# Another written order for a fused attention and expert kernel's first stage, and 21 small operations on another engine

## The chip, the cores and the metric

The kernel runs on one core of one Trainium2 chip. The metric is the device time of one execution in microseconds (us). A core has five engines with a queue each: TensorE (PE; its weight loads are PEld), VectorE (DVE), ScalarE (ACT), GpSimd (POOL) and SyncE (SP, which here only issues transfers). A queue runs in order: an instruction that waits holds up all behind it on its engine, and engines wait for one another through semaphores.

## The reference

Three steps follow one another, all in 32-bit floats.

```python
scores = scale * x @ state.T; a = softmax(scores); xread = a @ state        # B 4, H 8, S 512, Ns 32, D 64
scores2 = scale * state @ x.T; a2 = softmax(scores2); sread = a2 @ x
x = concat(xread, sread)                                                    # 2176 rows of 512
e = argmax(x @ w_gate); g = softmax(x @ w_gate)[e]                          # 8 experts, capacity 576
out = g * (relu(x @ w1[e]) @ w2[e])                                         # D 512, F 1024, rows over capacity give 0
h = out @ w_in; result = (h * clip(h + 3, 0, 6) / 6) @ w_out                # F 2048
```

## The kernel before

**Stages.** The function phase1 (line 72) is the first stage: attention, the choice of experts, the lists of rows for each expert, and, woven in, the first tile of 256 rows of the first expert. Then full (line 600) goes through the other expert tiles, with weights loaded as the routing asks for them, and at last through the dense layers (w_in, w_out), the longest stage. Every product of the expert and dense layers is made as three products of a high and a low part: the high part is a cast on ScalarE, the low part is the value minus the high part, on DVE or POOL.

**The first stage's parts.** Tiles are named by batch b (0 to 3) and half f (0, 1: four heads each). A part is a Python generator, and one step of it issues one or a few instructions:

- tr (269) turns x on TensorE and evicts it on ScalarE; scores (280) multiplies with the state into PSUM.
- soft_max (286) and turn (302) read the scores on DVE, soft_exp (296) on ScalarE. read_max (305) takes a maximum on DVE and subtracts it (L313: POOL, or DVE where ALT has sub), read_exp (315) is ScalarE's, read_sum (318) makes three DVE steps and a multiplication (L326: POOL, or DVE with mul in ALT). read_turn (328) turns the result on DVE.
- e2_turn (331), s_read (341), s_scale (357), s_turn (366) and s_logits (374) make sread and its logits. read (395) makes xread, evicted by ScalarE or, with rd in ALT, by DVE (L403). rows_out (407) adds up the logits and writes the rows to memory.
- count, total, sums, before and place (414 to 518) find each row's expert and its place in the list. first_expert (444) gives the index by which the first weights are loaded. before has one POOL copy (L513) ahead of two DVE sums.
- lists (520) makes, for five groups of rows of a batch, a pair of one-hot matrices: ol on DVE or ScalarE, oh (L538) on POOL or, with oh in ALT, on DVE. lists2 (542) multiplies the five pairs on TensorE (L544) and adds the result to the list LT on DVE.
- The parts that start with e_ (lines 941 to 1012) are the first expert tile: e_rows gathers its rows through two POOL transfers as soon as batch 0's list is there, e_x0 and e_x1 turn them, e_m0 to e_m3 are the first layer (L903, then ScalarE L907 and DVE L909), e_y0 and e_y1 the second (L921, then the product with the gate on DVE, L931, and the write to y_pad on SP, L937). w00 to w13 (L824, L826) split the first expert's eight weight blocks: a cast on ScalarE, then the low part on DVE or, with wp in ALT, on POOL.
- raws (835) loads these eight blocks on SP into four buffers, so the second four wait for the first to be used up. tables (662) and halves (711) are long rows of small DVE operations which say which tile belongs to which expert. inputs, setup0 to setup3, consts and zeros load and fill constants.

**What sets the order.** ORDER (line 29) is a list of part names, written out. Line 569 goes through it: each name advances that part by one step (name*3 by three), so it fixes the order of the instructions in each engine's queue. ALT (line 66) names the operations that go to the other of two engines.

**Behind the first stage** SP reads the tables and issues weight loads under conditions, POOL gathers the next tile's rows (L1133, L858) through the list, and TensorE turns them (L846). Where two tiles have one expert the load is left out.

Of the kernel before, what the change touches and what calls it, by code (L numbers as in the profile page):

```python
# [28 lines left out]
ORDER = """
    setup0 inputs setup0*4 tr00 prep_state0 tr01 tr00 setup2 setup3 prep_state0*2 tr01 scores00 setup2 tr02 setup3 setup2 setup0 tr03 setup2 setup0  # L30
    setup1 tr02 prep_state2 setup2*2 tr03 setup1*2 inputs*2 prep_state2 setup2*2 inputs prep_state2 soft_max00 prep_state2 scores01 prep_state2 tr10
    prep_state2 setup3*2 prep_gate soft_exp00 setup2 zeros turn00 read_max00 setup2*2 read_max00 setup2*2 read_exp00 soft_max01 turn01 setup2 setup3
    tr11 setup2*2 tr10 setup1 tr11 setup2 soft_exp01 read_max01 prep_gate e2_turn00 scores10 read_sum00 consts tr12 e2_turn00 s_read00 setup2
    e2_turn01 tr12 read_sum00*2 tr13 s_read00 setup2 soft_max10 read_max01 e2_turn01 tr13 s_read00 scores11 turn10 read_exp01 read_sum00 soft_exp10
    tr20 read_max10 inputs setup2 tr20 setup2 read_turn00 setup2*2 setup3 setup2 read_init0 read_sum01*2 soft_max11 read_sum01 read_init1 s_read01
    setup2 s_scale0 read06 read04 read_max10 turn11 read_exp10 soft_exp11 s_scale0 read_max11 tr21 tr22 tr21 read_sum01 scores20 setup3 tr23 s_read10
    read_sum10 setup3 s_read10 consts setup2 tr22 read04 read_sum10 e2_turn10 read_sum10 tr23 setup3 read_turn01 read_max11 read00 read_sum10 read06
    s_turn0 setup3 scores21 soft_max20 read_exp11 turn20 s_ids0 read05 read_turn10 read00 read_max20 turn21 read05 setup3 s_turn0 setup3 read_max20
    read_sum11 read01 read07 read01 read02 e2_turn10 read07 read03 soft_max21 s_logits0 read02 read03 read_exp20 read_max21 rows_out0 s_logits0 early
    read_sum11 count0 rows_out0 read_sum20 count0 e2_turn11 read10*2 count0 s_logits0 tr30 read_sum20 setup3 s_read10 e2_turn11 read_max21 count0 tr31  # L40
    setup3 s_scale0 setup3 read_sum11 setup3 count0 consts before0 setup3 tr30 read14 read_sum11 first_expert soft_exp20 read_exp21 first_expert tr31
    read_sum20 consts before0 read12 first_expert s_scale1 e2_turn20 read_sum21 first_expert*2 scores30 read_turn11 first_expert setup3 count0
    s_read11 setup3 first_expert before0 read_sum21 soft_exp21 s_read20 tr32 first_expert read_sum21 read15 read14 first_expert*2 raws total0 read12
    s_scale1 e2_turn20 tr32 soft_max30 s_read20 sums0 read13 place0 raws place0 e2_turn21 turn30 place0 read_sum21 read_turn21 s_turn1 read_sum20
    read13 tr33 place0 read_max30 raws read15 first_expert place0 e2_turn21 read16 read_turn20 place0 tr33 total0 place0 raws read_max30 place0
    s_read20 soft_exp30 s_scale2 read_init2 read11 scores31 s_logits0 s_turn1 place0 read17 lists0 e2_turn30 s_read21 read11 lists0 read16 read17 w00
# [1577 lines left out]
```

## Time and profile before

| | |
|---|---|
| median of 3 runs | 563.12 us (562.98 to 563.13) |
| the profiled execution | 564.15 us |
| its span | 562.4 us |
| mean granted TensorE clock | 0.978 of full speed |
| TensorE busy | 532.6 us, 95% of the span |
| DVE busy | 309.0 us, 55% |
| ScalarE busy | 218.0 us, 39% |
| POOL busy | 144.5 us, 26% |

A busy time is the sum of an engine's instructions. The span is the time from the first to the last instruction; the execution's own time has a little more around it. A share over the whole span is a mean over stages with different limits, so the rows further down are taken from stretches.

### The profile page before, as it was taken

Reading aid. Unit: us, or ns where it says so; the run is one execution under the profiler, and the core shown is the slowest. Engines: PE = TensorE matmul, PEld = TensorE weight load, DVE = VectorE, ACT = ScalarE, POOL = GpSimd, SP = SyncE. Lnnn points to the kernel's source line nnn. Section 1 sums busy time; section 2 is a strip of 40 time slices with the busy share of each in tenths; the row PEclk is TensorE's granted clock in tenths of the full one; section 3 lists DMA queues with packets and bytes.
Section 4 is the critical chain, followed back from the end, with each engine's and each line's share of the span. In section 5 each row is a group of like instructions: output and inputs, shape, how many; then the busy total and the mean of one; then the engine's idle time right before and its main releaser. Section 6 shows DMA issues by size and latency. Waiting matters only on the chain.

```text
span 562.4 us, 10121 instructions
## 1 busy us (share of the span) xinstructions
PE 532.6 (95%) x3772; PEld 466.5 (83%) x3772; DVE 309.0 (55%) x729; ACT 218.0 (39%) x461; POOL 144.5 (26%) x198
## 2 busy tenths in 40 slices
PE   5898899899999999999999999999999999999990
PEld 3566698796969898999998889999999998888880
DVE  3799978428735774676788953343334343222330
ACT  5577553225304250524444343333333343323340
POOL 1554645401610110117768732001001000000002
PEclk9798889999999999999999999999999999999997
DMA  6825730896989795336664312001001010000001
GB/s 136 184 103 218 247 111 20 281 401 232 374 283 401 251 377 174 98 113 226 224 209 148 115 37 76 1 23 53 1 19 58 1 31 19 20 0 1 0 13 57
DMA packets 52169, 74.99 MB, mean 133 GB/s; under 512 B 23089, under 2 KB 31537, under 8 KB 51602
## 3 DMA queue, kind: packets, MB, share of 16 engines
q1 hardware_dynamic: 49634, 66.83, 35.4%
q0 software_dynamic: 2208, 7.38, 3.9%
q8 instruction: 32, 0.52, 0.4%
q14 instruction: 23, 0.19, 0.1%
q10 hardware_dynamic: 272, 0.07, 0.1%
HBM read 70.62 MB, written 16.23 MB: 154 GB/s over the span
## 4 chain that ended last, share of the span: by engine, by line
issue 38%; PE 31%; DMA 15%; DVE 11%; ACT 3%; POOL 1%; POOLq 0%; SPq 0%; DVEq 0%; ACTq 0%
PE pm L921 8%; PE pm L903 7%; DMA out_dram<-o,fid 7%; DMA raw<-in_moe_w_dram 3%; DMA st<-in_moe_w_out_dram 3%; PE psX L400 2%; PE pm L1252 2%; PE p L1286 2%; PE pss L284 2%; PE pss L903 2%; DVE v L1096 1%; PE psx L276 1%; DVE g L1299 1%; DVE v L1094 1%; DVE v L1092 1%
## 5 line engine op out<-in xcount | busy, mean ns | idle before, releaser
L1286 PE MATMUL p<-yT,wh 128*128 128x256 f32 (+1 forms) x768 | 116.7, 294 | 0.0
L1286 PEld LDWEIGHTS p<-yT,wh 128*128 128x128 f32 x768 | 109.3, 188 | 7.8
L1299 DVE SCALAR_TENSOR_TENSOR g<-u,p 128x256 f32<-128x256 f32 x110 | 44.9, 409 | 111.0 <-ACT u L1298 110.9
L1298 ACT ACTIVATE u<-p,b 128x256 f32<-128x256 f32 x110 | 51.1, 464 | 103.4 <-PE p L1286 103.3
L1300 ACT CAST gh<-g 128x256 fp32r<-128x256 f32 x110 | 43.9, 399 | 79.9 <-DVE g L1299 79.9
L1464 POOL DMA_INDIRECT out_dram<-o,fid x14 | 14.0, 1000 | 215.9 <-ACT o L1463 190.8
L1286 PE MATMUL p<-yT,wl 128*128 128x256 f32 (+1 forms) x384 | 66.8, 296 | 0.9 <-POOL wl L1111 0.9
L1324 PE MATMUL po<-wh,gh 128*128 128x512 f32 x156 | 61.2, 392 | 0.0
L1324 PE MATMUL po<-wh,gl 128*128 128x512 f32 x156 | 61.2, 392 | 0.0
L1324 PE MATMUL po<-wl,gh 128*128 128x512 f32 x156 | 61.0, 391 | 0.0
L1286 PEld LDWEIGHTS p<-yT,wl 128*128 128x128 f32 x384 | 55.4, 189 | 2.6 <-POOL wl L1111 1.7
L1306 DVE TENSOR_TENSOR gl<-g,gh 128x256 fp32r<-128x256 f32 x84 | 34.4, 410 | 32.2 <-ACT gh L1300 32.2
L903 PE MATMUL pm<-xth,w1h 128*128 128x256 f32 x160 | 44.6, 283 | 1.8 <-ACT xth L849 1.5
L921 PE MATMUL pm<-hth,w2h 128*128 128x256 f32 x160 | 45.5, 284 | 0.0
L921 PE MATMUL pm<-hth,w2l 128*128 128x256 f32 x160 | 45.1, 282 | 0.0
L921 PE MATMUL pm<-htl,w2h 128*128 128x256 f32 x160 | 45.1, 282 | 0.0
L903 PE MATMUL pm<-xth,w1l 128*128 128x256 f32 x160 | 43.6, 277 | 0.0
L1111 POOL TENSOR_TENSOR wl<-v,wh 128x1024 fp32r<-128x1024 f32 x14 | 34.4, 2454 | 35.4 <-ACT wh L1110 35.0
L903 PE MATMUL pm<-xtl,w1h 128*128 128x256 f32 x160 | 41.6, 277 | 0.0
L1324 PEld LDWEIGHTS po<-wh,gl 128*128 128x128 f32 x156 | 29.3, 188 | 7.0 <-POOL gl L1306 0.6
L903 PEld LDWEIGHTS pm<-xth,w1h 128*128 128x128 f32 x160 | 30.1, 188 | 5.1 <-issue 2.9
L1306 POOL TENSOR_TENSOR gl<-g,gh 128x256 fp32r<-128x256 f32 x26 | 25.1, 967 | 30.6 <-ACT gh L1300 30.6
(307 smaller groups left out, 1029.1 us busy)
## 6 DMA issues: line engine op xcount, KB each, us to landing
raw<-in_moe_w_dram SPq DMA_DIRECT2D x80, 512.0 KB
st<-in_moe_w_in_dram SPq DMA_DIRECT2D x16, 512.0 KB
st<-in_moe_w_out_dram SPq DMA_DIRECT2D x16, 512.0 KB
x_rows<-xrow SPq DMA_DIRECT2D x4, 1072.0 KB
xb<-in_x_dram SPq DMA_DIRECT2D x32, 128.0 KB
yg<-y_pad SPq DMA_DIRECT2D x13, 258.0 KB
out_dram<-zt SPq DMA_DIRECT2D x2, 1536.0 KB
y_pad<-y SPq DMA_DIRECT2D x5, 516.0 KB
```

Of the source, the lines that this page charges most:

```text
L284: T.matmul(ps[64 * a:64 * a + 64, :], sT[:, 2 * b + f, 64 * a:64 * a + 64], st[b]["xT"][:, 2 * f + a], start=True, stop=True)
L400: T.matmul(ps, s["aT"][:, f, j, :], bd[:, 2 * b + f, :], start=True, stop=True)
L903: T.matmul(ps[:, j], W1[l][k][:, ls], xT[r][:, k], start=n == 0, stop=n == 11)
L921: T.matmul(ps[:, j], W2[l][k // 2][:, k % 2, ls], hT[k // 2][r][:, k % 2], start=k == 0 and i == 0, stop=k == 7 and i == 2)
L1111: (V if m in (0, 2) else G).tensor_tensor(out=wl, in0=v, in1=wh.bitcast(F32), op=ALU.subtract)
L1286: T.matmul(out, w[:, 128 * k:128 * k + 128], r(k), start=n == 0, stop=n == 11)
L1298: A.activation(out=u, in_=ps, func=AF.Relu, bias=b3)
L1299: V.scalar_tensor_tensor(out=g, in0=u, scalar=6.0, in1=ps, op0=ALU.min, op1=ALU.mult)
L1300: A.copy(gh[:, 0:w], g)
L1306: eng.tensor_tensor(out=gl, in0=g[:, 0:n], in1=gh[:, 0:n].bitcast(F32), op=ALU.subtract)
L1324: T.matmul(po[t], l[:, ls], r[:, 512:1024], start=m == 0 and i == 0, stop=m == 15 and i == 2)
L1464: G.indirect_dma_start(out=out, out_offset=bass.IndirectOffsetOnAxis(ap=fid[0:n, t:t + 1], axis=0), in_=o[0:n], in_offset=None, bounds_che ...
```

## The change

ORDER is written anew from the first word to the last; every part occurs as often as before. ALT changes in 21 names. From DVE to POOL go the multiplications mul11 and mul30, the subtraction sub30 and the one-hot rows oh01, oh12, oh20 and oh34. From POOL to DVE go mul21, sub10, oh04, oh31 and the low parts of w01, w03 and w11 (wp). From DVE to ScalarE go the evictions rd10, rd17, rd21, rd31 and rd37; from ScalarE to DVE go rd01 and rd27. Here are the lines of it that are spoken of below:

```diff
@@ -27,45 +27,44 @@
 SCALE = 0.125
 
 ORDER = """
-    setup0 inputs setup0*4 tr00 prep_state0 tr01 tr00 setup2 setup3 prep_state0*2 tr01 scores00 setup2 tr02 setup3 setup2 setup0 tr03 setup2 setup0
-    setup1 tr02 prep_state2 setup2*2 tr03 setup1*2 inputs*2 prep_state2 setup2*2 inputs prep_state2 soft_max00 prep_state2 scores01 prep_state2 tr10
-    prep_state2 setup3*2 prep_gate soft_exp00 setup2 zeros turn00 read_max00 setup2*2 read_max00 setup2*2 read_exp00 soft_max01 turn01 setup2 setup3
-    tr11 setup2*2 tr10 setup1 tr11 setup2 soft_exp01 read_max01 prep_gate e2_turn00 scores10 read_sum00 consts tr12 e2_turn00 s_read00 setup2
...
-    read27 lists0 s_logits1 s_scale1 read_exp30 lists0 read24 lists0 read27 read25 lists0 rows_out1 s_scale2 turn31 soft_max31 lists0*2 s_ids2
-    soft_exp31 s_logits1 read_max31 s_turn2 read26 read25 lists0 count1 lists0*3 read24 first_expert lists20 count1 read26 read_sum30 consts read23
-    lists20 s_read30 count1 read_max31 read20 e_rows read_exp31 read_sum30 s_read30 e2_turn31 s_turn2 read23 e2_turn30 count1 read20 e_rows read_sum30
-    read21 e2_turn31 count1 read_sum31 rows_out1 before1 read_sum30 s_read30 s_logits2 read_sum31 count1 w01 read_turn30 consts read22 read_init3
...
-    read30 w02 read33 s_scale3 read31 e_x0 read36 e_x1 e_x0 s_scale3 e_ok before1 s_turn3 place1 read35 read33 rows_out2 total1 read37 raws count2
-    before1 count2 e_g s_turn3 w01 e_x1 s_logits1 read36 w03 s_logits1 e_x1 read37 s_logits3 read35 s_logits3 place1 count2 rows_out3 e_m0 count2
-    place1 count2 e_m0 place1 e_m0 count3 e_m0 place1 count3 e_m1 e_g place1*2 w10 count2 e_m0 s_logits2 place1*2 count3 total2 e_m0 before2 count3
-    before2 count3 total2 lists1 e_m0 s_ids3 count3 lists1*2 e_m1*2 total3 sums3 before2 before3 total3 raws lists1 before3 lists1 e_g sums2 before3
-    w10 lists1 e_m1 totals e_m0 place2 tables e_m1*2 e_m2 lists1 e_g place3 rows_out2 lists1 e_m2*3 e_ok e_m2 place2 tables place2 lists1 place2 e_m1
...
-    place2 e_m3 halves w13 lists2 place2 halves w11 w13 e_y1 lists2*5 s_scale2 e_ok tables halves lists21 e_y1 lists2 halves e_y0 place3 lists2 halves
-    lists2*2 tables halves lists2 tables e_y0*3 halves lists2 e_y0 tables halves place3 lists22 lists3*2 halves*2 lists3 tables lists3 e_g halves
-    lists3*2 e_y0 s_logits2 lists3 halves lists3 e_y1 lists22 e_y0 s_logits3 lists3*2 halves*2 lists3*2 tables halves lists3 e_g halves tables*2
-    lists23*2 halves e_gt*2 e_y1 halves e_y0 e_y1 halves e_y0 e_y1*2 halves e_y1 halves*3 e_y1*2
+    setup0*2 inputs tr00 setup0*4 tr01 setup0 tr00 prep_state0 setup2 setup1 setup2 prep_state0 zeros tr01 setup2 consts*2 setup2*2 prep_state0 setup1
+    inputs prep_state2 scores00 tr02 setup1 inputs tr02 setup2 tr03 tr10 setup2 tr03 setup3 setup2*2 scores01 prep_state2 soft_max00 tr11 prep_state2
+    turn00 read_max00*2 tr10 turn01 read_max01 prep_state2 setup3 soft_exp00 soft_max01 e2_turn00 tr11 setup2 read_exp00 prep_state2 setup3 e2_turn00
+    read_sum00 scores10 soft_exp01 soft_max10 read_max01 setup3*2 read_exp01 prep_state2 tr12 setup1 tr13 setup2 prep_gate tr12 tr13 read_sum00 inputs
...
+    read10 s_ids1 read_exp30 read10 place0 first_expert place0 turn31 e2_turn21 place0*3 read13 place0 s_turn1 s_logits1 s_logits0 total0 e2_turn21
+    s_logits1 read13 lists0 place0*2 soft_exp30 read15*2 read11 lists0 s_read20 read11 s_read21 read_sum21 rows_out1 lists0 soft_exp31 lists0*3 read26
+    s_scale2 read_max31 consts raws count1 read_max31 e2_turn30 read_turn21 read26 lists0 read_sum30 raws lists0 read_exp31 lists0 count1 read_sum30
+    lists0 rows_out1 s_scale2 s_logits0 e2_turn31 s_read30 read25 lists0 read27 count1 s_scale1 read24 read_sum30 read25 lists0 read_sum30 s_ids2
+    read_sum31 lists20 read27 lists20 e2_turn31 read24 read23 read22 s_read30 w00 read23 s_turn2 read22 read_sum31 e_rows s_read31 count1 read20
+    read21 e2_turn30 e_rows read_turn30 s_turn2 read_init3 s_read30 count1 read_sum31 s_logits2 w02 count1 read_sum31 read20 before1 read32 w00
...
+    total1 raws count2 s_scale3 consts e_x0 w01 s_logits1 e_x0 read35 e_x0 s_turn3*2 e_g before1 count2*2 e_x1 before1 read34 read36 rows_out2
+    s_logits3 place1*2 read35 read37 e_x1 s_logits3 count2 e_x1 s_logits1 w03 count2 place1 read33 w03 w10 place1*2 count2 read33 e_m0 total2 e_m1*2
+    read36 e_m0 before2 e_m0 read37 sums2 e_m0 w10 rows_out3 e_m0 e_g total2 place1 count3 place1 e_m0 count3*2 place2 before2 count3 e_m1 place1 e_ok
+    first_expert w12 e_m1 e_m0 e_g count3 lists1 e_m1*2 count3 before2 before3*2 e_g total3 place2 total3 e_m0 totals sums3 raws w12 e_m2 place3
+    lists1 e_g place1 before3 e_g s_logits3 e_m2 place2 e_m2 place2 tables raws place2 e_m1 tables lists1 w11 e_m2 e_m1 e_m2 place3 e_g e_m2 w11 e_m3
+    s_ids3 place3 tables e_m3 s_logits2 e_g lists1 e_m3 lists1 e_m3 tables lists1 e_m2 place2 lists1*2 tables e_m3 lists1*2 tables halves tables
...
+    s_scale2 s_logits3 lists2*4 e_y0 lists2 lists21 lists2 e_y1 place3 halves lists2 halves e_y1 tables halves lists2 tables place3 e_y1 tables
+    lists2*4 place3 e_y1 halves lists22 tables halves lists3 s_logits2 halves lists22 halves tables e_y0 lists3 halves lists3 halves lists3 halves
+    lists3 tables halves e_y0 e_y1 lists3*6 halves tables halves lists3 tables lists3 lists23 e_y1 halves*2 rows_out3 lists23 e_gt e_y0 halves*2 e_y0
+    tables s_scale3 halves e_y1 halves e_y0 e_y1 e_y0 e_y1 halves e_y1 halves
 """
 
 
 ALT = frozenset("""
-    mul11 mul30 mul31 oh01 oh12 oh20 oh30 oh32 oh34 ol01 ol02 ol10 ol11 ol12 ol21 ol22 ol30 ol33 ol34 rd10 rd17 rd21
-    rd31 rd37 sub30 wp01 wp03 wp11
+    mul21 mul31 oh04 oh30 oh31 oh32 ol01 ol02 ol10 ol11 ol12 ol21 ol22 ol30 ol33 ol34 rd01 rd27 sub10
 """.split())
```

Read from left to right, some places differ as follows. turn00 stands ahead of soft_exp00, where it stood behind it. scores01 stands behind tr10, where it stood ahead of it. Between read_max31 on DVE and the one-hot row ol03 stand read_turn21 and the first step of read_sum30. read_sum31's first step stands ahead of e_rows. On POOL the multiplication of read_sum30 stands ahead of e_rows' two transfers. On DVE w00, w02 and w01 stand ahead of the low parts of e_x0 and e_x1, and w03 behind them; w12 and w11 follow between the first layer's parts. On POOL before2 and before3 stand ahead of all one-hot rows of lists1 to lists3, so that twelve of these follow one another. On TensorE lists21 stands ahead of e_y0's first step, and lists22 and lists23 between steps of e_y0 and e_y1.

## Rows read from the trace of the kernel before

**Rows 1.** Stretches: length, busy us of PE, PEld, DVE, ACT, POOL (instructions); PEclk, DMA share, GB/s

```profile
14.00:57.00 43.00, 39.24 (x433) 26.35 (x432) 37.83 (x115) 30.81 (x77) 22.82 (x63) 0.88 0.56 168
...
67.50:98.50 31.00, 30.06 (x223) 29.17 (x221) 25.53 (x128) 13.54 (x28) 14.20 (x26) 0.90 0.28 96
98.50:128.50 30.00, 27.22 (x224) 25.58 (x224) 11.29 (x22) 8.74 (x15) 6.19 (x12) 1.00 0.95 338
128.50:562.00 433.50, 420.10 (x2784) 374.75 (x2780) 218.70 (x437) 152.25 (x316) 91.03 (x69) 0.99 0.34 117
```

**Rows 2.** Chain of waits, 57 to 129 us: start, length, what

```profile
61.07 4.40 DVE w1l L826 x2
...
67.58 7.12 PE pss L903 x36
...
95.52 3.53 DMA xg<-x_rows,col
...
118.04 10.31 DMA raw<-in_moe_w_dram
```

**Rows 3.** Timeline of SP's queue: start, length, instruction, count

```profile
101.39 0.39 SPq L937 DMA_DIRECT2D y_pad<-xb  x1
...
105.12 13.25 SPq L814 DMA_DIRECT2D raw<-in_moe_w_dram  x16
```

**Rows 4.** Waits of DVE, 9.49 to 53.6 us: total, times, longest

```profile
DVE R L303 <- ACT e L300: 3.1, 1, 3.1
DVE m L294 <- PE pss L284: 1.8, 2, 1.4
DVE rs L320 <- ACT R L316: 0.8, 1, 0.8
DVE rr L348 <- ACT e L300: 0.7, 2, 0.4
DVE t L485 <- PE bank L478: 0.6, 1, 0.6
```

**Rows 5.** Timeline of PE, 11 to 14 us: start, length, instruction [idle before, releaser]

```profile
11.06 1.22 PE L284 MATMUL pss<-xT,sT 128*64 128x512 f32 x4
13.29 0.63 PE L276 MATMUL psx<-identk,xb 128*128 128x128 f32 x4 [1.01 <-DMA xb<-in_x_dram]
```

**Rows 6.** Timelines of DVE and POOL: long operations beside one another

```profile
50.65 1.85 DVE L536 TENSOR_SCALAR ol<-io,lo,idmi 32x128 fp32r<-32x128 f32 x1
...
57.81 2.64 DVE L439 TENSOR_TENSOR Gs<-Gs,O 128x8 f32<-128x8 f32 x1
...
82.34 1.78 DVE L718 SCALAR_TENSOR_TENSOR Q<-Q,c 128x8 f32<-128x8 f32 x1
...
58.07 2.35 POOL L826 TENSOR_TENSOR w1l<-raw,w1h 128x1024 fp32r<-128x1024 f32 x1
```

**Rows 7.** Groups by line, 0 to 98.5 us: count, busy us, mean ns, idle before

```profile
L826 DVE TENSOR_TENSOR w2l<-raw,w2h 128x1024 fp32r<-128x1024 f32 x3 | 3.7, 1222 | 0.0
...
L326 POOL TENSOR_TENSOR R<-R,rs 128x512 f32<-128x512 f32 x5 | 5.2, 1049 | 5.7 <-ACT xT L278 2.1 <-DVE Gs L465 1.8 <-DVE rs L324 1.3
...
L326 DVE TENSOR_TENSOR R<-R,rs 128x512 f32<-128x512 f32 x3 | 2.1, 685 | 0.0
...
L538 POOL TENSOR_SCALAR oh<-io,hi 128x144 fp32r<-128x144 f32 (+1 forms) x14 | 11.0, 794 | 7.7 <-DVE hi L507 3.2 <-DVE Q L657 2.6 <-DVE s L747 1.0
...
L538 DVE TENSOR_SCALAR oh<-io,hi 128x144 fp32r<-128x144 f32 (+1 forms) x6 | 2.1, 354 | 0.0
```

**Rows 8.** Timelines of PE at 86 us and of DVE at 100 us

```profile
86.15 0.38 PE L921 MATMUL pss<-xb,w2h 128*128 128x256 f32 x1 [0.77 <-DVE xb L909]
...
100.60 0.69 DVE L931 TENSOR_TENSOR xb<-pss,gB 128x512 f32<-128x512 f32 x1 [3.38 <-PE pxt L846]
```

**Rows 9.** Timelines of DVE and POOL around 54.6 us

```profile
54.66 0.68 DVE L326 TENSOR_TENSOR R<-R,rs 128x512 f32<-128x512 f32 x1
...
54.58 1.28 POOL L858 DMA_INDIRECT xb<-x_rows,ecol  x1 [2.16 <-PE psX L400]
```

More of the change, by code (lines that the diff above doesn't have):

```diff
@@ L34 @@
[L34 to L45, printed above, removed]
@@ L50 @@
-    read21 e2_turn31 count1 read_sum31 rows_out1 before1 read_sum30 s_read30 s_logits2 read_sum31 count1 w01 read_turn30 consts read22 read_init3
-    read22 read34 read_sum31 w02 read21 read32 read_sum31 read32 s_ids1 read30 read34 s_logits2 total1 read_turn31 w00 s_read31 sums1 e_x0 w03 read31
-    read30 w02 read33 s_scale3 read31 e_x0 read36 e_x1 e_x0 s_scale3 e_ok before1 s_turn3 place1 read35 read33 rows_out2 total1 read37 raws count2
-    before1 count2 e_g s_turn3 w01 e_x1 s_logits1 read36 w03 s_logits1 e_x1 read37 s_logits3 read35 s_logits3 place1 count2 rows_out3 e_m0 count2
@@ L58 @@
-    e_g*2 e_m3 e_m2 e_m3 raws halves consts e_m2 tables e_ok s_logits3 w11 place3 halves s_scale3 lists1 place3 e_m3 lists21 tables halves tables
-    place2 e_m3 halves w13 lists2 place2 halves w11 w13 e_y1 lists2*5 s_scale2 e_ok tables halves lists21 e_y1 lists2 halves e_y0 place3 lists2 halves
-    lists2*2 tables halves lists2 tables e_y0*3 halves lists2 e_y0 tables halves place3 lists22 lists3*2 halves*2 lists3 tables lists3 e_g halves
-    lists3*2 e_y0 s_logits2 lists3 halves lists3 e_y1 lists22 e_y0 s_logits3 lists3*2 halves*2 lists3*2 tables halves lists3 e_g halves tables*2
@@ new lines @@
+    read_sum00 scores10 soft_exp01 soft_max10 read_max01 setup3*2 read_exp01 prep_state2 tr12 setup1 tr13 setup2 prep_gate tr12 tr13 read_sum00 inputs
+    e2_turn01 setup3 scores11 setup3 s_read00 turn10 read_sum01*2 read_max10 setup3*2 tr20 consts s_read00*2 read_sum00 setup2 e2_turn01 read_max10
+    read_sum01 tr21 soft_exp10 setup3 soft_max11 setup2 read_exp10 turn11 setup2 setup3 read_sum01 s_read01 read_sum00 tr20 tr22 setup2*2 early setup2
+    read_sum10 tr21 setup2*2 scores20 read_max11 tr23 read_turn01 read_max11 soft_exp11 tr22 prep_gate setup3 e2_turn10 setup2 setup3 s_scale0 read01
@@ new lines @@
+    soft_max20 read_turn00 setup2 s_scale0 s_turn0 tr23 read_sum10 setup2 s_read10 setup2 scores21 consts setup2 turn20 read_sum10 read00 read_init0
+    s_turn0 read_sum10 e2_turn10 e2_turn11 read_exp11 read01 read03 read_max20 read05 read00 turn21 e2_turn11 read03 read06 read05 read_sum11
+    s_logits0 read_max21 read04 read02 read_sum11 s_logits0 setup2 soft_exp20 read_max20 read06 s_read10 read07 inputs read_exp20 read04 read_sum11
+    read02 read_turn10 read07 soft_max21 read_init1 read_max21 read_sum20 read_sum11 read_exp21 s_read10 rows_out0 tr30 tr31 read_sum20 read16
@@ new lines @@
+    count0*3 read_sum20 count0 soft_exp21 count0 setup3 read_sum21 tr31 s_read11 read_turn11 read12 first_expert before0 s_scale0 first_expert
+    read_sum21 tr30 tr32 first_expert scores30 before0 first_expert count0 first_expert before0 first_expert*2 tr33 read_sum20 read_sum21 first_expert
+    read12 setup3*2 tr32 tr33 s_read20 soft_max30 setup2 e2_turn20 turn30 s_ids0 read17 first_expert read16 s_scale1 read_max30 rows_out0 raws read17
+    total0 scores31 setup3*2 read_max30 s_scale1 e2_turn20 read14 raws read_turn20 setup3 s_turn1 soft_max31 sums0 place0 read14 read_init2 s_read20
@@ new lines @@
+    read_sum31 lists20 read27 lists20 e2_turn31 read24 read23 read22 s_read30 w00 read23 s_turn2 read22 read_sum31 e_rows s_read31 count1 read20
+    read21 e2_turn30 e_rows read_turn30 s_turn2 read_init3 s_read30 count1 read_sum31 s_logits2 w02 count1 read_sum31 read20 before1 read32 w00
+    first_expert e_ok total1 read_turn31 read21 s_scale3 read30 rows_out2 read32 consts sums1 raws read31 w01 w02 read34 read30 read31 s_logits2 e_ok
+    total1 raws count2 s_scale3 consts e_x0 w01 s_logits1 e_x0 read35 e_x0 s_turn3*2 e_g before1 count2*2 e_x1 before1 read34 read36 rows_out2
@@ new lines @@
+    s_ids3 place3 tables e_m3 s_logits2 e_g lists1 e_m3 lists1 e_m3 tables lists1 e_m2 place2 lists1*2 tables e_m3 lists1*2 tables halves tables
+    place3 place2 e_m2 halves lists1*3 place3 e_m3 e_gt place2 lists21 halves e_y0 tables e_m3 place2 place3 e_ok w13 halves e_y0 e_m3 halves w13
+    s_scale2 s_logits3 lists2*4 e_y0 lists2 lists21 lists2 e_y1 place3 halves lists2 halves e_y1 tables halves lists2 tables place3 e_y1 tables
+    lists2*4 place3 e_y1 halves lists22 tables halves lists3 s_logits2 halves lists22 halves tables e_y0 lists3 halves lists3 halves lists3 halves
```

2 lines of the change are left out of this document (removed).

## The prediction

> **What bounds the kernel now.** I read the stretches first, then the chain of waits, then the queues' timelines, and the means by line for prices. The stretches [rows 1] show a last stage of 433 us in which TensorE is busy 420: nothing that the change touches lies there, and it can only begin sooner or later. Ahead of it lie 30 us, from 98.5 to 128.5, with the DMA engines busy 0.95 of the time: weights of the next experts. The chain [rows 2] says what starts them. DVE's two low parts of W1 (ending 65.5) release TensorE's run on the first expert tile (67.6 to about 98.5); that and the gather of the next tile's rows (95.5 to 99.05), which needs the finished list, end together; then the weights come (118.0 to 128.4). SP issues the output of the first tile at 101.4 and the 16 load instructions behind it from 105.1 [rows 3]. So the 30 us of loads start when the first stage ends: a microsecond gained at the stage's end is a microsecond of the whole, through the loads and the last stage. The question is what the new order and the 21 moved operations do to the stage's end. In it DVE is the fullest engine up to 67.5 (37.8 of 43 us between 14 and 57) and TensorE from there on (30.1 of 31) [rows 1].
>
> **How the new order is read.** Each word of ORDER advances one part by one step, and each step's engine stands in its function, so the queue of each engine is had by reading ORDER from left to right. No part has more or fewer steps than before. I compare how much work stands ahead of three points in each queue: the gather of the first tile's rows (e_rows), the start of e_m0 on TensorE, and the last list (lists23).
>
> **Term A, up to e_rows: 3.5 us gained.** Before 53.6 DVE waited 3.1 us for ScalarE's exp of the first tile and 1.8, 0.8, 0.7 and 0.6 us elsewhere, 7.0 in these five rows [rows 4]. The 3.1 arise because turn00 stands behind soft_exp00; now it stands ahead of it. But scores01, which ran at 11.06, now stands behind tr10 in TensorE's queue, and tr10 waited for its input until 13.29 [rows 5]: scores01 would end at 13.29 + 0.63 + 1.22 = 15.1, and turn01 waits for it. I credit nothing for the 3.1. What is gained is that tile 00's subtraction (POOL) and exp (ScalarE) run inside that wait, and that e2_turn00 reaches TensorE with its input ready, so that the waits of 1.8, 0.8 and 0.7 (3.3) can go. A second gain: ol04 took 1.85 us [rows 6] right after read_max31 let POOL start its subtraction; a one-hot pass of similar width takes 0.35 [rows 7], so 1.5 were blocked. Now two 512-wide passes stand between. Against it, read_sum31's pass of 0.69 [rows 7] moves ahead of e_rows. 3.3 + 1.5 - 0.7 = 4.1, and I take 3.5, since some new wait must appear. Of the swaps in this stretch, two 512-wide passes leave DVE (mul11, sub30) and two come (mul21, sub10), 0.69 each; two evictions and one one-hot row leave, as many come: nothing net, covered by DVE itself. Ends: a loss of 2.2 (11.06 to 13.29, if the late scores01 is never made up for) and a gain of 7.0 + 1.5 - 0.7 = 7.8.
>
> **Term B, e_rows to e_m0: 2.3 us gained.** A DVE sum of 8 elements took 2.64 us at 57.81 while POOL made w01's low part (58.07, 2.35 long) [rows 6]: charged 0.15 for itself, 2.5 were blocked. DVE's own two low parts took 4.40 in the chain [rows 2] beside POOL's w03; without POOL such a pass takes 1.22 [rows 7], so 2.0 come back. Now DVE makes all four: w01 and w03 cost 2 x 1.22 = 2.4 more. mul30 leaves (0.7), and read21 and read31 (264 columns, between 0.35 for 144 and 0.69 for 512 [rows 7]; I take 0.5 each). As w03 now stands behind e_x1's low part, DVE must wait for ScalarE's casts; I charge the 0.8 + 0.7 that it waited for ScalarE in [rows 4]. 2.5 + 2.0 - 2.4 + 0.7 + 1.0 - 1.5 = 2.3. Ends: 0 if the casts take it all, 3.8 without that wait. The w2 loads wait for w00 to w03 to be used up, so they move with them. Behind the waiting w03 stand w10 and the counts of tiles 2 and 3; TensorE's queue reaches the sums made of these only after several groups of e_m0.
>
> **Term C, TensorE's run: 0.3 gained.** TensorE stood still once, 0.77 us at 86.15, for a DVE low part [rows 8] behind an 8-element DVE operation that took 1.78 [rows 6] while POOL made w11's low part. w11 now costs DVE 1.22 and saves those 1.6; the stall goes (+0.8). Against it, oh12, oh20 and oh34 go to POOL, and only oh31 comes off it in this stretch (oh30 and oh32 stay on DVE). A POOL row takes 0.79 against 0.35 [rows 7], list 2 is now wholly POOL's, and its matmuls stand inside e_y in TensorE's queue, so a late row holds TensorE. I charge 0.5. Ends: a loss of 3.2 (four rows at 0.79 in TensorE's way) and a gain of 0.8.
>
> **Term D, the end of the stage: 1.2 gained.** The last product of the tile on DVE began at 100.60, released by the transposes [rows 8], which waited for the gather to land at 99.05 [rows 2], though TensorE's run was over near 98.5. With POOL's w11 gone and the tables and lists no later in DVE's queue, the gather should be ahead of TensorE's end. At most 100.60 - 98.5 = 2.1 go; at least 0.
>
> **Sum.** 3.5 + 2.3 + 0.3 + 1.2 = 7.3. The profiled execution took 564.15 us (span 562.4, 1.75 around it); 564.15 - 7.3 = 556.85. The median of the runs is 563.12, 1.03 below that execution, so I predict 555.8 for the median. Next late thing: TensorE's own run, then the loads, both unchanged.
>
> **A rule weighed.** While POOL's w01 pass lasted, DVE's sum did not end [rows 6]; it had begun first, by 0.26 us. The Trainium skill ("SBUF — State Buffer", Who interferes with whom) says that a DVE instruction with two SBUF inputs, or in a two-port mode, and a GpSimd instruction that reads SBUF exclude each other: whichever starts first has the shared ports for its whole length. The trace agrees that DVE loses about POOL's whole pass, not on the stated order of the starts. By that rule the passes moved to POOL speak against the change, and it is the second rival below.
>
> **Rivals.** (1) **DVE becomes the bound behind e_m0.** It was busy 25.5 of 31 us there [rows 1]; the change takes 1.6 of blocking and three one-hot rows (1.1) off, and adds w11 and most of w03 (2.4) and oh31 (0.35): 25.5 again. If it needs the 5.5 idle us too, the list ends only half as much sooner as e_m0 starts, and 3.5 of the gain is lost: 559.3. For: DVE waits for TensorE in this stretch. Against: the counts come earlier in the queue.
> (2) **The moved passes hold DVE up.** Three 512-wide passes of 1.05 on POOL (sub30, mul11, mul30) and four one-hot rows of 0.79 [rows 7], each blocking DVE for its length, with nothing from those that leave POOL: 3.15 + 3.16 = 6.3, so 562.1. For: ol04's 1.85. Against: POOL loses three low parts and four other passes.
> (3) **The gathers wait for mul30: slower.** On POOL mul30 now stands ahead of e_rows' gathers. On DVE it started at 54.66 and the gathers at 54.58 [rows 9]. If term A gains nothing, mul30 on POOL ends at 54.66 + 1.05 = 55.7 and the gathers start 1.1 late; e_x1 follows them, and w03's 1.22 stands behind it on DVE: 2.3 later, 565.4. It decides as soon as read_sum30's sum is no earlier than it was.
> (4) **Nothing moves.** The loads' start hangs on something else and hides the gain: 563.1. The chain speaks against it.
>
> **How the numbers follow.** My forecast has 0.62, the rivals 0.17, 0.08, 0.09 and 0.04. A measurement of this kernel can tell about 0.2%, 1.1 us. Faster by more than that are the forecast and (1): 0.79; within it (2) and (4): 0.12; slower (3): 0.09. The range, 551.0 to 562.2: at the top it takes in (1) and (2), at the bottom a gain 4.8 beyond my sum, which term A's and B's upper ends allow together (4.3 + 1.5 more). What is left out is (3), (4) and sums of several bad ends.
>
> **What the profile after would show.** No POOL instruction at L826 in the first stage, and DVE's eight there at about 1.2; no 8-element DVE operation above 1 us. The e_rows gathers near 51, e_m0's first matmul near 61.7, with about 31 us to the last of e_y1; SP's y_pad issue near 94. Wrong would be: e_m0 at 67 or later; TensorE waiting at L544 for POOL's L538 by more than a microsecond; the y_pad issue earlier by several microseconds with the total unmoved.

## The result and the profile after

The changed kernel took a median of 560.68 us (20 executions, 553.78 to 563.22), the kernel before 563.19 beside it. The ratio is 0.9893, with a 95% interval of 0.9863 to 0.9924; it is taken of the fast runs alone, without the five of the changed kernel from 562.1 us up, and so is not the quotient of the two medians, 0.9955. The kernel is faster, as forecast; the median lies inside the range, 4.9 us above the forecast of 555.8.

The executions fall into two groups: 9 of the 20 took 553.8 to 555.7 us, 11 took 560.4 to 563.2. The profile shown as after belongs to the longer group (562.41 us, span 560.2). A second profile of the same kernel, called **again** here (557.36 us, span 555.1), belongs to the shorter. The two first part at the gathers, which is the main finding below. Which group holds the median is a matter of two executions.

| us from the start | before | after | again |
|---|---|---|---|
| first gather of e_rows issued | 54.58 | 54.18 | 53.87 |
| first matmul of e_m0 | 67.51 | 68.53 | 61.92 |
| last matmul of e_y1 ends | 98.63 | 96.39 | 89.50 |
| SP issues y_pad | 101.39 | 97.95 | 90.66 |
| span | 562.4 | 560.2 | 555.1 |

**The start.** The stretches of after that answer to the first and third line of [rows 1]; its timelines of ScalarE, VectorE and TensorE at the start; and two lines from those of the kernel before:

```profile
14.00:57.00 43.00, 42.88 (x503) 29.26 (x502) 38.46 (x120) 35.84 (x90) 24.24 (x66) 1.00 0.56 168
...
67.50:98.50 31.00, 29.25 (x230) 27.91 (x228) 25.66 (x126) 14.08 (x30) 15.44 (x24) 0.97 0.24 78
```

```profile
0.83 1.28 ACT L155 ACT_TABLE_LOAD   x1 [0.83 <-PEq L1605]
...
7.23 0.43 ACTq L135 DMA_DIRECT2D aT<-in_state_dram  x1
...
9.85 0.23 DVE L161 COPY aT<-aT 128x128 f32<-128x128 f32 x1 [6.72 <-DMA aT<-in_state_dram]
...
14.76 0.69 DVE L293 TENSOR_REDUCE m<-pss 128x1 f32<-128x512 f32 x1 [1.72 <-PE pss L283]
...
12.73 1.97 PE L283 MATMUL pss<-xT,sT 128*64 128x512 f32 x4 [0.16 <-DVE sT L252]
```

```profile
0.83 0.43 ACTq L136 DMA_DIRECT2D aT<-in_state_dram  x1
...
9.49 0.69 DVE L294 TENSOR_REDUCE m<-pss 128x1 f32<-128x512 f32 x1 [0.44 <-PE pss L284]
```

ScalarE's transfer of the state was its first instruction before, issued at 0.83. `setup0*2 inputs` puts it behind the table load and a small exp, which end at 2.33; it goes out only at 7.23. The trace does not say what it waited for; the program as built has, in this place of ScalarE's queue, a wait for another transfer's completion, which is not there before and not in state_first below. VectorE waits 6.72 us for the state, the first scores run at 12.73 instead of 7.43, and the maximum of tile 00 at 14.76 instead of 9.49: 5.3 us lost. The gathers start 0.4 earlier than before all the same, so the new order won back 5.7 us between the two points. TensorE, busy 39.2 us from 14 to 57 before, is now busy 42.9, and its granted clock there is 1.00 (2.4 GHz); before, it was 0.88 in the mean, with 0.50 (1.2 GHz) from 16 to 20 us, behind 4 us in which TensorE was busy 2.5.

**The gathers.** The timelines of GpSimd, VectorE, SP and TensorE, first of after, with one stretch (columns as in [rows 1]) at its end, then of `again`:

```profile
54.18 2.33 POOL L857 DMA_INDIRECT xb<-x_rows,ecol  x1 [0.81 <-PE bank L353]
...
56.81 1.40 POOL L857 DMA_INDIRECT xb<-x_rows,ecol  x1 [0.30 <-issue]
...
54.14 1.22 DVE L825 TENSOR_TENSOR w1l<-raw,w1h 128x1024 fp32r<-128x1024 f32 x1
...
56.12 1.22 DVE L825 TENSOR_TENSOR w1l<-raw,w1h 128x1024 fp32r<-128x1024 f32 x1
...
55.39 2.46 SPq L813 DMA_DIRECT2D raw<-in_moe_w_dram  x2
...
59.95 0.63 PE L845 MATMUL psc<-identk,xb 128*128 128x128 f32 x4 [1.96 <-DMA xb<-x_rows,ecol]
...
64.52 1.12 PE L845 MATMUL psc<-identk,xb 128*128 128x128 f32 x4 [3.38 <-DMA xb<-x_rows,ecol]
...
68.53 0.78 PE L902 MATMUL pss<-xT,w1h 128*128 128x256 f32 x1
...
64.00:66.00 2.00, 1.48 (x6) 1.25 (x6) 0.64 (x5) 0.33 (x1) 0.00 (x0) 0.50 0.96 377
```

```profile
53.87 1.28 POOL L857 DMA_INDIRECT xb<-x_rows,ecol  x1 [0.87 <-PE bank L353]
...
55.45 1.00 POOL L857 DMA_INDIRECT xb<-x_rows,ecol  x1 [0.30 <-issue]
...
53.88 1.25 DVE L825 TENSOR_TENSOR w1l<-raw,w1h 128x1024 fp32r<-128x1024 f32 x1
...
55.95 1.23 DVE L825 TENSOR_TENSOR w1l<-raw,w1h 128x1024 fp32r<-128x1024 f32 x1
...
55.16 2.54 SPq L813 DMA_DIRECT2D raw<-in_moe_w_dram  x2
...
57.67 0.63 PE L845 MATMUL psc<-identk,xb 128*128 128x128 f32 x4
...
59.74 0.66 PE L845 MATMUL psc<-identk,xb 128*128 128x128 f32 x4 [0.89 <-DMA xb<-x_rows,ecol]
...
61.92 0.47 PE L902 MATMUL pss<-xT,w1h 128*128 128x256 f32 x1
```

In after the low part of w00 began at 54.14, 0.04 us ahead of the first gather, and the gather took 2.33 us. In `again` the gather began at 53.87, 0.01 us ahead of the low part, and took 1.28, as before [rows 9]. The second gather met w02's low part in the same way: 1.40 against 1.00. From their starts the gathers took 5.6 and 7.7 us to land in after, 3.7 and 4.2 in `again`, and e_m0 began 6.6 us apart. Of these, 4.8 are there when the second gather's rows reach TensorE (64.52 against 59.74). The other 1.8 are the clock: in after TensorE had stood still from about 61 to 64.5 and was granted 0.50 (1.2 GHz) from 64 to 68, and its four transposes took 1.12 us instead of 0.66; in `again` the clock was 1.00 up to e_m0. state_first's profile, below, is of its shorter group and shows the same tie: gather and low part both begin at 50.08, and the gather took 1.28.

**TensorE's run and the end.** The stretches of `again` that answer to the third line of [rows 1], and the chain behind them, with one line of the chain of after at the end; then, of the kernel before, one short stretch that explains the 0.90 there. Columns as in [rows 1]; those of the chain as in [rows 2]:

```profile
61.90:89.50 27.60, 26.95 (x223) 26.10 (x221) 24.19 (x120) 13.76 (x30) 13.58 (x22) 1.00 0.32 113
...
93.50:99.50 6.00, 5.92 (x28) 5.95 (x29) 1.29 (x8) 0.64 (x2) 2.35 (x4) 0.51 0.96 299
...
93.58 5.46 PE pm L902 x24
...
127.49 2.94 PE pm L902 x24
...
99.88 4.59 PE pm L902 x24
```

```profile
68.00:70.00 2.00, 2.00 (x11) 2.00 (x11) 1.97 (x17) 0.92 (x1) 0.32 (x2) 0.50 1.00 399
```

Before, TensorE's run from e_m0 to e_y1 took 31.1 us, with the granted clock at 0.50 (1.2 GHz) from its beginning to 73; just ahead, from 64 to 66, TensorE had been busy 0.13 of the 2 us. In `again` it took 27.6 at a granted clock of 1.00. SP's queue of after and of `again`, which answers to the first line of [rows 3], and the groups of VectorE's low parts in after, which answer to [rows 7]:

```profile
97.95 0.39 SPq L936 DMA_DIRECT2D y_pad<-xb  x1
```

```profile
90.66 0.39 SPq L936 DMA_DIRECT2D y_pad<-xb  x1
```

```profile
L825 DVE TENSOR_TENSOR w1l<-raw,w1h 128x1024 fp32r<-128x1024 f32 x4 | 4.9, 1217 | 0.0
```

All eight low parts of this stage are on VectorE, four of W1 and four of W2, at 1.21 to 1.34 us each.

### The profile page after: what moved, and what is told of

It reads as the page before. It is cut to its first block, busy times and chain, and to the rows that moved or that the text cites. A ratio compares the mean times of both kernels' runs of the same rounds, so it can differ in the third digit from the quotient of the medians.

```text
span 560.2 us, 10116 instructions
## 1 busy us (share of the span) xinstructions
PE 530.2 (95%) x3772; PEld 464.8 (83%) x3772; DVE 301.0 (54%) x726; ACT 219.1 (39%) x464; POOL 138.9 (25%) x198
## 4 chain that ended last, share of the span: by engine, by line
PE 55%; issue 15%; DVE 5%; DMA 5%; ACT 1%; POOL 1%; POOLq 0%; DVEq 0%; ACTq 0%
PE p L1285 15%; PE po L1323 14%; PE pm L920 10%; PE pm L902 10%; DMA st<-in_moe_w_out_dram 2%; DMA out_dram<-o,fid 2%; PE pm L1251 2%; PE pm L1225 2%; DVE v L1095 2%; DVE g L1298 1%; DVE v L1091 1%; DMA st<-in_moe_w_in_dram 1%; DVE v L1093 1%; ACT wh L1109 1%; PE pxt L845 1%
## 5 line engine op out<-in xcount | busy, mean ns | idle before, releaser
L902 PE MATMUL pm<-xth,w1h 128*128 128x256 f32 x160 | 45.5, 288 | 0.7 <-POOL col L1191 0.7
L902 PE MATMUL pm<-xth,w1l 128*128 128x256 f32 x160 | 44.4, 281 | 0.0
L902 PE MATMUL pm<-xtl,w1h 128*128 128x256 f32 x160 | 42.2, 281 | 0.0
L1323 PEld LDWEIGHTS po<-wh,gl 128*128 128x128 f32 x156 | 29.2, 187 | 7.0 <-POOL gl L1305 0.4
L902 PEld LDWEIGHTS pm<-xth,w1h 128*128 128x128 f32 x160 | 30.9, 193 | 3.8 <-issue 2.1
L1323 PEld LDWEIGHTS po<-wh,gh 128*128 128x128 f32 x156 | 29.3, 188 | 3.8
```

The costliest lines, as they stand in the source:

```text
L902: T.matmul(ps[:, j], W1[l][k][:, ls], xT[r][:, k], start=n == 0, stop=n == 11)
L1323: T.matmul(po[t], l[:, ls], r[:, 512:1024], start=m == 0 and i == 0, stop=m == 15 and i == 2)
```

## The experiments

In each, "stretch" is the time from e_m0's first matmul to the first gather of the next tile's rows: 28.0 us before (67.51 to 95.52), 24.9 in after (68.53 to 93.44), 24.8 in `again` (61.92 to 86.74).

**state_first**, the state's transfer ahead of the table load:

```diff
-    setup0*2 inputs tr00 setup0*4 tr01 setup0 ...
+    setup0 inputs setup0 tr00 setup0*4 tr01 setup0 ...
```

> The changed kernel with one word of ORDER moved: inputs stands ahead of the second setup0 again, so ScalarE issues the first state transfer before its table load, at 0.8 us as before the change, not at 7.2. Theory: in the changed kernel that transfer waits for the completion of SP's own state transfer, which costs 5.3 us at the first scores (12.73 against 7.43); with the word back the first scores run near 7.5 and the whole is about 5 us shorter, 550 to 557 by whichever of the two groups of times it falls into. Rival: DVE and the other engines make the late start good before the first expert tile, and the time stays within 1 us of the changed kernel's 555 or 561.

558.73 us (552.41 to 560.38), ratio 0.9912 (0.9868 to 0.9956). Two groups as well: 552.4 and 553.1, and four at 558.2 to 560.4. In its profile (span 550.7) the transfer goes out at 0.83 and the first gather at 50.08, 3.8 us ahead of `again`'s. So the start's loss is real. In the whole it costs 3.2 to 3.4 us in either group against the executions of `again`, taken beside these (medians of the groups 552.8 against 556.1 and 559.6 against 562.8), and 2.0 to 2.3 against those of after; less than at the gather either way. Not all came back: the first scores ran at 8.76, not near 7.5, and the longer group lies above the expected 550 to 557.

**w2_behind**, the four W2 loads and two later transfers moved in SP's queue behind the third step of s_logits1:

```diff
-    ... sums1 raws read31 ... total1 raws count2 ... sums3 raws w12 ... tables raws place2
+    ... sums1 read31 ... total1 count2 ... s_logits1 s_scale2 s_scale3 raws*4 w03 ... sums3 w12 ... tables place2
```

> The changed kernel with the four transfers of the first expert's W2 moved in SP's queue behind the row writes of tiles 2 and 3 (last steps of s_scale2 and s_scale3 moved ahead of them). Theory: the earlier low parts of W1 set free their buffers at 55 to 59 us, so W2 is loaded while the two gathers of the first tile's rows are in flight (5.6 and 7.7 us from issue to landing against 3.6 and 4.7 before the change); with W2 behind, the gathers land within 4 to 5 us, e_m0 starts near 64 to 65, not 68.5, and the times form one group near 555 with none above 559. Rival: the two groups of times (555 and 561) come from TensorE's granted clock alone; then both groups remain and the gathers' landing does not change the end.

563.07 us (560.83 to 565.81), ratio 0.9990 (0.9963 to 1.0016): the gain was gone. The timelines of GpSimd and SP, and VectorE's longest wait:

```profile
53.37 1.50 POOL L857 DMA_INDIRECT xb<-x_rows,ecol  x1 [0.87 <-PE bank L353]
...
55.17 1.00 POOL L857 DMA_INDIRECT xb<-x_rows,ecol  x1 [0.30 <-issue]
...
55.09 0.34 SPq L411 DMA_DIRECT2D x_rows<-xrow  x1
...
64.73 2.31 SPq L813 DMA_DIRECT2D raw<-in_moe_w_dram  x4
...
DVE w2l L825 <- ACT w2h L823: 3.5, 1, 3.5
```

The idea that the W2 loads alone make the longer group fell. The gathers were hardly stretched, yet landed after 4.2 and 6.1 us: rows_out2, 1072 KB, had moved up to 55.09, into the place of the first two W2 loads (512 KB each). And the W2 loads at 64.73 were too late for VectorE.

**state_w2**, both edits:

> Both moves together: inputs first, W2's transfers behind. Theory: the two losses lie at different places and add up, so the time is about 5 us below w2_behind's, near 549 to 551. Rival: with the start 5 us earlier something else gates the gathers (ScalarE's evictions of tile 1, POOL's passes), and the gain over the better of the two single moves is under 2 us.

559.23 us (556.41 to 560.33), ratio 0.9924 (0.9897 to 0.9952), no better than state_first, so the two moves do not add up. Its use is the gathers (timelines of GpSimd and VectorE, the first gather):

```profile
50.70 2.00 POOL L857 DMA_INDIRECT xb<-x_rows,ecol  x1 [0.94 <-PE psX L399]
...
50.33 1.22 DVE L825 TENSOR_TENSOR w1l<-raw,w1h 128x1024 fp32r<-128x1024 f32 x1
```

**again**, the changed kernel unaltered:

> The changed kernel itself, for a profile of the shorter of its two groups of times (554 to 556) beside the one of the longer (560 to 563). Theory: in the short group the gathers of the first tile's rows land 4 us or more sooner and TensorE's clock does not fall between 62 and 70 us. Rival: the start differs (the state transfer lands earlier than 9.9 us).

562.04 us (555.99 to 563.86), ratio 0.9955 (0.9914 to 0.9995); three executions at 556.0 to 557.4, five at 561.7 to 563.9. The groups are the kernel's own. Its profile is read above; as its theory had it, the clock does not fall from 62 to 70 us; the state reaches VectorE at 9.80, as in after (9.85), so the start is not the difference.

The held gathers now gave a rule in numbers. In after the pass at 54.14 ends at 55.36, 1.18 us behind the gather's start, and the gather took 1.05 over its 1.28. In state_w2 the pass ends at 51.55, 0.85 behind the start, and the excess is 0.72. In w2_behind it is a 512-wide product that ends 0.35 behind the start, and the excess is 0.22. Each time the excess is the rest of the pass, less 0.13. A pass with one input did not do this: in `again` a transpose of VectorE from 55.20 to 55.90 lay over the second gather's start, and that gather took 1.00. Three experiments followed from it.

**low_late**: w00 and w02 behind the sums that follow them, w01 behind e_x0's copy:

```diff
-    ... read32 w00 first_expert ... w01 w02 read34 ... e_x0 w01 s_logits1 e_x0 read35 e_x0 s_turn3*2
+    ... read32 first_expert ... w01 read34 ... e_x0 w00 w02 s_logits1 e_x0 read35 e_x0 w01 s_turn3*2
```

> The changed kernel with VectorE's low parts w00 and w02 moved in its queue behind the sums that follow them, and w01 behind the copy of e_x0, so that no two-input pass of 128x1024 stands beside the gathers of e_rows. Theory (a pass of VectorE that has begun when GpSimd's gather starts holds the gather to the pass's end): gathers of 1.28 and 1.00 us in every execution, e_m0 near 62, one group of times at 554 to 557, median near 555.5. Rival (the W2 loads stretch the gather): half the executions still at 560 to 563, or a gather over 1.3 us. Rival (the later low parts hold TensorE): one group, but at 557 to 560, with TensorE waiting for VectorE at L902.

556.54 us (555.72 to 557.75), ratio 0.9878 (0.9855 to 0.9901). One group. The timelines of GpSimd, SP and TensorE:

```profile
53.45 1.28 POOL L857 DMA_INDIRECT xb<-x_rows,ecol  x1 [0.87 <-PE psX L399]
...
58.32 1.23 SPq L813 DMA_DIRECT2D raw<-in_moe_w_dram  x2
...
61.04 0.48 PE L902 MATMUL pss<-xT,w1h 128*128 128x256 f32 x1
```

Taking the passes away from the gathers removed the longer group. The first W2 loads moved too, from 55.2 to 58.3, because they wait for w00 and w02 to be used up; low_late alone does not separate the two.

**first_late**, low_late with state_first's edit:

> low_late, and the state's transfer issued by ScalarE ahead of its table load, as in state_first. Theory: both gains add up, one group at 551 to 554, median near 552.5, with y_pad near 87. Rival: two groups remain, near 552.5 and 559, as state_first had.

553.80 us (552.27 to 555.39), ratio 0.9819 (0.9795 to 0.9843): faster than both kernels, and one group. The two gains add up. Its first gather took 1.43 us, held 0.15 by the rest of a 512-wide product, with no W2 load before 55.48, and the landings took 3.6 to 3.8.

**held**, w00 one instruction earlier in VectorE's queue of the changed kernel:

```diff
-    ... s_logits2 w02 count1 read_sum31 read20 before1 read32 w00
+    ... s_logits2 w02 count1 w00 read_sum31 read20 before1 read32
```

> The changed kernel with VectorE's low part w00 one instruction earlier in its queue, ahead of the last softmax product, so that it has always begun when GpSimd's gather starts. Theory (the gather is held to the pass's end, and then meets the W2 loads): a first gather of 1.6 to 1.9 us instead of 1.28 in the profile, the executions in the longer group, 559 to 563. Rival (chance, or the loads alone, set the group): again two groups, or all at 554 to 557 with a gather of 1.28.

562.86 us (556.42 to 564.24), ratio 0.9971 (0.9949 to 0.9993); 11 of 12 executions at 561.8 to 564.2, one at 556.4. The timelines of GpSimd, VectorE and TensorE:

```profile
53.12 1.26 POOL L388 COPY xsc<-idss 32x1 f32<-32x1 f32 x1 [1.22 <-DMA x_rows<-xsc]
...
54.55 1.55 POOL L857 DMA_INDIRECT xb<-x_rows,ecol  x1 [0.17 <-PE psX L399]
...
56.39 1.40 POOL L857 DMA_INDIRECT xb<-x_rows,ecol  x1 [0.30 <-issue]
...
53.13 1.21 DVE L825 TENSOR_TENSOR w1l<-raw,w1h 128x1024 fp32r<-128x1024 f32 x1
...
54.26 0.68 DVE L325 TENSOR_TENSOR R<-R,rs 128x512 f32<-128x512 f32 x1
...
67.56 0.48 PE L902 MATMUL pss<-xT,w1h 128*128 128x256 f32 x1
```

The gather was held, though not by w00, but by the product behind it: it ends at 54.94, 0.39 behind the gather's start, and the excess is 0.27. w00 held the small copy ahead of the gather, 1.26 us instead of 0.17, so that the gather started 0.7 later than in `again`. The first W2 loads went out at 54.36. The gathers were 0.27 and 0.40 too long; with all that the landings took 5.6 and 7.4 us, and e_m0 began at 67.56. That is more than the hold itself, and it goes with the megabyte that SP sends then. How much of held's shift is due to the W2 loads being 0.8 earlier than `again`'s was not taken apart.

**order_alone** and **engines_alone**, the change's two halves:

```diff
-    mul21 mul31 oh04 oh30 oh31 oh32 ol01 ol02 ol10 ol11 ol12 ol21 ol22 ol30 ol33 ol34 rd01 rd27 sub10
+    mul11 mul30 mul31 oh01 oh12 oh20 oh30 oh32 oh34 ol01 ol02 ol10 ol11 ol12 ol21 ol22 ol30 ol33 ol34 rd10 rd17 rd21
+    rd31 rd37 sub30 wp01 wp03 wp11
```

This is order_alone against after; engines_alone is the change without the ORDER lines of its diff.

> The new order with every operation on the engine that it had before. Theory (order and engines add up: the order gives what was gained ahead of e_rows, 1.1 us, the engines the rest): 561 to 563, GpSimd's low parts w01, w03 and w11 at about 2.4 us again and an 8-element pass of VectorE of over 2 us beside one. Rival (the order pays alone): 558 or less. Rival (the order needs the engines): over 564, with VectorE waiting for GpSimd ahead of 52 us.

> The order of before with the 21 operations on their new engines. Theory (they add up): the start keeps its 0.83 us issue, no low part on GpSimd, 2 to 4 us gained between e_rows and the lists: 559 to 561. Rival (they need the new order): 562.5 or more, because w03's low part stands in VectorE's queue ahead of e_x1's.

order_alone: 560.60 us (559.56 to 561.76), ratio 0.9939 (0.9916 to 0.9962). engines_alone: 568.68 (566.99 to 571.76), ratio 1.0096 (1.0070 to 1.0122), slower than before by 4.6 us; its profile is of the fastest of its six executions. They do not add up. order_alone is a little better than the theory of adding up had it, and shows the long passes of that theory; of engines_alone the rival was right on the time, but the largest wait is another than the one it named. VectorE and GpSimd in order_alone:

```profile
59.11 1.83 DVE L440 TENSOR_TENSOR Gs<-Gs,O 128x8 f32<-128x8 f32 x1
...
73.22 2.45 DVE L666 TENSOR_SCALAR co<-co,capk 128x8 f32<-128x8 f32 x1
...
58.47 2.45 POOL L825 TENSOR_TENSOR w1l<-raw,w1h 128x1024 fp32r<-128x1024 f32 x1 [0.61 <-ACT w1h L823]
...
73.27 2.36 POOL L825 TENSOR_TENSOR w2l<-raw,w2h 128x1024 fp32r<-128x1024 f32 x1
```

The first row ends at 60.94, GpSimd's pass at 60.92; the second at 75.67 and 75.63. With a third such row (63.29, 2.21 long) about 6 us of VectorE's time go, TensorE waits 2.1 us for VectorE at L902, and the stretch is 29.2 us instead of 24.9. In engines_alone:

```profile
DVE aT L328 <- POOL R L325: 3.3, 1, 3.3
...
58.52 1.04 POOL L325 TENSOR_TENSOR R<-R,rs 128x512 f32<-128x512 f32 x1
```

In the old order the gathers start at 55.77, 1.2 us later than before; ahead of them VectorE waits 1.7 us for TensorE at an eviction that came to it (49.80). The product that went to GpSimd stands behind both gathers there, at 58.52, and VectorE waits 3.3 us for it. The stretch is 29.3 us.

**late_wp**, **late_oh** and **late_soft**: low_late with one kind of operation back on its old engine:

```diff
-    mul21 mul31 oh04 oh30 oh31 oh32 ... rd01 rd27 sub10
+    mul21 mul31 oh04 oh30 oh31 oh32 ... rd01 rd27 sub10 wp01 wp03 wp11
...
-    mul21 mul31 oh04 oh30 oh31 oh32 ... rd01 rd27 sub10
+    mul21 mul31 oh01 oh12 oh20 oh30 oh32 oh34 ... rd01 rd27 sub10
...
-    mul21 mul31 oh04 oh30 oh31 oh32 ... rd01 rd27 sub10
+    mul11 mul30 mul31 oh04 oh30 oh31 oh32 ... rd10 rd17 rd21 rd31 rd37 sub30
```

> low_late with the low parts w01, w03 and w11 back on GpSimd. Theory (their move is what shortened the stretch from e_m0's first matmul to the gather of the next tile, 28.0 us before, 29.2 in order_alone, 25.3 in low_late): about 29 us in that stretch, 559.5 to 562. Rival (the one-hot rows did it): the stretch stays at 25 to 26 and the time at 555.5 to 557.5.

> low_late with the six one-hot rows back on the engines that they had before. Theory (low parts): 555.5 to 557.5, the stretch from e_m0 to the gather at 25 to 26. Rival (one-hot rows): 559 or more, the stretch at 28 or more, TensorE waiting at L543 for a row.

> low_late with the softmax steps (sub, mul) and the evictions (rd) back on the engines that they had before. Theory (they are nothing net, as the prediction had it): 555.5 to 557.5, e_rows' first gather within 0.7 us of low_late's 53.45. Rival (the order needs them): the gather at 54.5 or later and 558 or more.

late_wp: 560.91 us (558.33 to 562.49), ratio 0.9931 (0.9910 to 0.9952), 4.4 us over low_late. late_oh: 556.91 (556.52 to 557.76), ratio 0.9871 (0.9854 to 0.9889), the same as low_late, though its stretch, 26.5 us, is above the 25 to 26 expected. late_soft: 560.06 (558.12 to 561.52), ratio 0.9928 (0.9908 to 0.9947), 3.5 us over low_late. Of late_wp, VectorE's low parts and GpSimd's; of late_soft, TensorE's longest wait:

```profile
56.67 4.66 DVE L825 TENSOR_TENSOR w1l<-raw,w1h 128x1024 fp32r<-128x1024 f32 x2
...
57.90 2.35 POOL L825 TENSOR_TENSOR w1l<-raw,w1h 128x1024 fp32r<-128x1024 f32 x1
```

```profile
PE pss L902 <- DVE xT L850: 2.1, 1, 2.1
```

VectorE's two low parts took 4.66 us beside GpSimd's pass, where two take 2.4 alone. The stretch of late_wp is 31.0 us, above order_alone's 29.2, so a part of its 4.4 us comes from low_late's later place for w00 and w02, which there meets GpSimd's w01. The softmax steps and evictions were not "nothing net": with them back, the gather starts at 55.05, 1.6 us later than in low_late, and TensorE waits 2.1 us for VectorE.

## Why the prediction was right, and where it failed

**The frame held in its number, not in its reason.** A microsecond at the stage's end is nearly one of the whole. The first gather of the next tile and the span lie 467 us apart before (95.52, 562.4), in after (93.44, 560.2), in low_late (86.29, 553.6) and in engines_alone (97.51, 564.7). But of these chains only that of before goes through the loads; in after and `again` the chain runs through TensorE from the next tile's first matmul on (99.88 and 93.58). "Then the loads, both unchanged" missed that TensorE itself comes next, though it was busy 27.2 of those 30 us before [rows 1]. Its first 24 matmuls there took 5.46 us in `again`, at a granted clock of 0.51 behind 4 us in which TensorE was busy 1.3, and 4.59 in after, against 2.94 for the same 24 later, and a part of the gain stays there: `again` issues y_pad 10.7 us earlier than before and ends 7.3 earlier, after 3.4 and 2.2. state_first reaches the next tile's gather earlier than `again` (83.17 against 86.74), took 4.39 for the 24, and passed on 11.7 of its 12.4 us there, where `again` passed on 7.3 of 8.8.

**Term A, forecast 3.5, was 0.4 (after) and 0.7 (`again`).** Inside the stretch the order gained more than forecast: 5.7 behind the late start, and 4.5 with the state's transfer back in its place (state_first, 50.08). A part of it may be the clock, which the term did not price: 0.88 from 14 to 57 before [rows 1], 1.00 in after and in order_alone. The step that failed is the count of what is moved: the rule that every transfer of a moved step counts was not applied to `inputs`, whose first transfer stands in ScalarE's queue. That lost 5.3 at the first tile, more than the whole loss of 2.2 at the term's lower end. state_first confirmed it. The swaps of softmax steps and evictions, costed at nothing, are worth 1.6 us at the gather beside low_late's other moves (late_soft); all 21 moves together brought it forward by 0.1 to 0.4 (54.24 in order_alone).

**Term B, forecast 2.3, was 4.9 in `again` and -1.4 in after.** From the gather to e_m0 it took 12.93 us before, 8.05 in `again`, 14.35 in after. What the term said of GpSimd's passes was right: with them gone no 8-element operation of VectorE took over 0.76 us, and late_wp and order_alone brought the long ones back. What failed is the sentence "the w2 loads wait for w00 to w03 to be used up, so they move with them". It left unpriced that the gathers would share their time with these loads and with w00's low part. By its own sign of being wrong, "e_m0 at 67 or later", the longer group (68.53) fails the forecast, though the median lies in the range. The profiles say how the two go together. The first landing took 3.6 to 4.2 us wherever the first gather ended no later than SP sent its first 512 KB or more: at the same moment in `again` and state_first, 0.2 to 0.7 us ahead in w2_behind and order_alone, well ahead in low_late, first_late and the three runs built on low_late. It took 5.6 to 7.1 where the gather ended later than that: by 1.1 in after, 0.9 in state_w2 and 1.7 in held. Between after and `again` the loads moved by 0.2 us and the gather's end by 1.4, so there it is the hold that makes the difference. low_late and held agree with it, each with a second thing moved.

This step and the start together are why the median lies 4.9 us above the forecast. That it lies in the range is in part luck. The range's upper part was there for rivals 1 and 2, and neither came. In the shorter group the time comes within 1 us of the forecast, but from terms of 0.7, 4.9, 3.5 and 1.6, of whose sum of 10.7 only 7.3 reached the end.

**Term C, forecast 0.3, was 3.3 (after) and 3.5 (`again`).** The stall of 0.77 at 86.15 [rows 8] went, as forecast, and moving the one-hot rows cost nothing in the median (late_oh). The mis-sized part is the clock. Before, TensorE's run had a granted clock of 0.90 over 31 us [rows 1], which is 3.1 us if all of it counts; in `again` it was 1.00 over 27.6. The term took the clock in TensorE's run as fixed.

**Term D, forecast 1.2, was 1.2 (after) and 1.6 (`again`):** from the last matmul of e_y1 to the issue of y_pad 2.76 us before, 1.56 and 1.16 now. VectorE's last product no longer waits for the transposes: in after it starts at 96.97, 0.1 ahead of the first of them.

**The rivals.** (1) VectorE did not become the bound behind e_m0: TensorE's run was shorter than before, not longer. (2) The passes moved to GpSimd held VectorE nowhere for long: in after no operation of VectorE other than a low part took over 0.76 us from 14 to 100. (3) did not arise: in after the product on GpSimd began at 51.23 and was over well before the gathers. engines_alone is slower, but not by this rival: there the product stands behind the gathers, and VectorE waits for it. (4) fell.

**The rule on the shared ports.** In nine gathers of these profiles a pass of VectorE with two inputs in SBUF had begun first, and held the gather to the pass's end; where the gather had begun first, as in `again`, it was not held. The Trainium skill ("SBUF — State Buffer", Who interferes with whom) says that the one that issues first decides who is blocked. For the gathers the trace agrees. It does not for order_alone's row at 73.22, nor for the copy in held: by the recorded starts each began first, by 0.05 and 0.01 us, and yet ended with the other engine's pass.

What stays open: why the landing behind a held gather grows from about 4 to 5.6 and 7.7 us. A late start alone does not do it: in late_soft the gathers began at 55.05 and 56.63 with no W2 load before 61.48, and landed after 3.6 to 3.8. The growth fits the megabyte that SP sends in after, held, state_w2 and w2_behind, but no run had a gather held for long with SP silent.

## What to carry to other kernels

When a step is moved, list every queue that it issues to: one transfer behind a table load cost 5.3 us at the first tile here, and 2 to 3.4 of the whole. Two instructions on engines that can block one another, begun 0.01 to 0.04 us apart, went with a kernel of two times here; putting one clearly behind the other, which also moved the W2 loads, left one time and took 4 us off the median. A move of operations between engines is worth what the order makes of it: the same 21 moves cost 4.6 us in the old order, and gained about 4 in the new one where the gathers were not held (560.60 in order_alone, 556.0 to 557.4 in `again`'s shorter group), and nothing by the median of all executions (560.68).
